# Block-sparse attention and a gated MLP on one core: another mask setup, and transposes, values and evictions of the first batch in other places

## The chip, the core and the metric

The kernel runs on one core of a Trainium2 chip. Its engines work side by side, each through its own instructions in order: TensorE (PE in the profile; its weight loads are PEld), VectorE (DVE), ScalarE (ACT), GpSimd (POOL) and SyncE (SP), whose queue issues most of the DMAs. An instruction that needs another engine's result waits on a semaphore, and all that is queued behind it on its engine waits too. The metric is the device time of one execution in microseconds (us), less being better.

## The reference

Attention over 4 batches of 8 heads, 768 positions, head size 64, with a mask of 24 x 24 blocks of 32 positions (the neighbours, the first and last rows and columns of blocks, and three sampled blocks in each row), and then a gated MLP with a product over the positions:

```python
scores = scale * np.matmul(q, k.transpose(0, 1, 3, 2))
scores = np.where(mask, scores, -1000000000.0)
...
x = softmax(scores) @ v            # heads side by side: batch, 768, 512
h = np.maximum(x @ w_in, 0.0)
u, v = h[..., :512], h[..., 512:]
v_n = (v - mean(v)) / np.sqrt(var(v) + 1e-06)
v_s = np.einsum('ts,bsd->btd', w_spatial, v_n) + b_spatial
return (u * v_s) @ w_out
```

## The kernel before

**The mask inside the product.** The tile `kq` holds, for each of 8 heads, keys and queries transposed: partitions 0 to 63 are the head's 64 numbers, partitions 64 to 87 (`MR`) are 24 rows of mask. In the key columns (`K_`) these rows are a one-hot of the key's block; in the query columns they hold 0 or -300 for each block. One product over 88 partitions so gives scores with the mask added. The query's mask rows are `bm` (24 x 24, written by DVE at L203) times the one-hot of the keys: `mask_rows` (L266) makes such a product of 256 columns, "a third", into PSUM, and copies it to head 0. `rows` (L233) copies mask rows from head 0 to other heads, on ACT, POOL or DVE.

**The front.** ACT and SP issue the first loads. PE runs 26 products on a tile of zeros (`filler`, L174), so that it is busy while the first keys come. DVE builds one-hot (L195, into head 0) and `bm`. ACT casts the first keys and copies the one-hot to heads 1 and 2. PE transposes the first keys of head 0 (`head`, L272), DVE copies them to `kq` (`split0`, L278), and the first queries of head 0 follow in the same way into `psq`. After that come the three mask products, m0, m1 and m2; m0 and m1 have as their moving operand whole columns of `kq`, so they wait for the keys' copies; m2 takes the 24 mask rows alone. ACT copies m0 and m1 out, DVE m2. 5, 2 and 1 fillers stand between (`FILL2`), and 5 more in slot 2 (`FILL3`).

**The stream.** `ORDER` (L302) is the order in which POOL casts the rest of batch 0: `k`, `q`, `v` and a number name the keys, queries or values of a pair of heads; a, b, c are the first third, the last two thirds or the last third of the queries; `r` stands for a copy of mask rows; w00 to w13 are pieces of w_in. SP issues the loads in the same order, four ahead. v3 stands behind q0c and q3b.

**The slots.** Batch 0 runs in 36 slots (`S0`). Slot 3u+e makes a piece of the scores of unit u: four products (L397) and one exponential on ACT (L402). Two PSUM tiles take turns for the scores. Units 0 and 1 are heads 0 and 1, units 2 to 4 the first query third of pairs 1 to 3, units 5 to 7 the second, units 8 to 11 the third. The product with the values (L443, eight matmuls for each slot) comes later: unit 2 in slots 10 to 12, unit 3 in 12 to 14, unit 4 in 15 to 17, unit 5 in 18 to 20. Its result stands in one of two PSUM tiles (tag `av`). DVE normalizes it (L425, L426), PE transposes it back into the same tile (`xtr_third`), and DVE copies it to `xt` (L208). Only then is the tile free, so the value product of unit 4 waits for the copy to `xt` of unit 2, and that of unit 5 for unit 3's.

Within a slot the order is scores, then what `pre` holds, value products, what `when` put there, MLP steps (`run_queue`), and what `late` holds. `tr_first(p)` transposes a pair's keys and its first query third (8 on PE, two copies of 1024 columns on DVE); `tr_rest(p)` does the other two thirds (4 on PE, two copies of 512 columns). They stand in slots 4, 6, 10 and in slots 8, 11, 15 for pairs 1, 2, 3. A copy of mask rows on DVE (heads 4 to 7, second and third query third) is in slot 14. From slot 36 on the other batches go through full heads (L410, L414, L461), with the MLP of the batch before in between (L547). The last product of a batch's MLP is copied out of PSUM by `o_product` (L640), ACT and DVE by turns, six copies in a batch.

Of the kernel before, what the change touches and what calls it, by code (L numbers as in the profile page):

```python
# [10 lines left out]
FP32 = mybir.dt.float32  # L11
# [3 lines left out]
ALU = mybir.AluOpType  # L15
# [11 lines left out]
def kernel(  # L27
# [16 lines left out]
    nc = tc.nc  # L44

    B, H, S, D = q.shape
    BLK = 32
    NB = S // BLK
    NR = sampled_blocks.shape[1]
    NCH = S // 128  # L50
# [10 lines left out]
    KR = D + NB  # L61
    NT = 3
    TC = NCH // NT
    TW = TC * 128
    S0 = NT * NG * 3
    FILL, FILL2, FILL3 = 26, (5, 2, 1), 5
    U_DVE = (0, 1, 2, 3, 4, 5)

    const = ctx.enter_context(tc.tile_pool(name="const", bufs=1))
# [1 line left out]
    psum = ctx.enter_context(tc.tile_pool(name="psum", bufs=1, space=bass.MemoryType.PSUM))  # L71
# [10 lines left out]
    kq = const.tile([KR, H, 2 * S], BF16, name="kq")  # L82
    NVV = 6
    vv = [const.tile([128, 2, NCH, VA], BF16, name=f"vv{s}") for s in range(NVV)]
    MR = slice(D, KR)
    K_, Q_ = slice(0, S), slice(S, 2 * S)

    def qcols(t0, n=1):
        return slice(S + t0 * TW, S + (t0 + n) * TW)
# [9 lines left out]
    H0, H1, BOTH = slice(0, 1), slice(1, 2), slice(0, 2)  # L99
# [16 lines left out]
    def cast(p, nm, eng, hs=BOTH, cs=ALLC):  # L116
        if nm == "v":
            dst = vv[p % NVV][:, hs, cs, 0:D]
        else:
            if p not in nat:  # L120
                nat[p] = work.tile([128, 2 * NCH, 2, D], BF16, tag="nat", bufs=4, name="nat")
            c0 = 0 if nm == "k" else NCH
            dst = nat[p][:, c0 + cs.start:c0 + cs.stop].rearrange("p c h d -> p h c d")[:, hs]
        src = st[nm, p].rearrange("p h (c d) -> p h c d", d=D)[:, hs, cs]
        if p == 0 and nm != "v":
            dst = nat0_view()[:, hs, (c0 + cs.start) * D:(c0 + cs.stop) * D]
            if cs is not C45:
                dst = dst[:, 0].rearrange("p (i t d) -> p t i d", t=2, d=D)
                src = src[:, 0].rearrange("p (t i) d -> p t i d", t=2)
            else:  # L130
                dst = dst.rearrange("p h (c d) -> p h c d", d=D)
        if eng is nc.scalar:
            nc.scalar.activation(out=dst, in_=src, func=AF.Copy)
        else:
            eng.tensor_copy(out=dst, in_=src)  # L135
# [13 lines left out]
    hot = const.tile([KR, NCH, 128], BF16)  # L149
    lim = const.tile([KR, NCH, 128], BF16)  # L150
    allow = const.tile([KR, NB], FP32)
    bm = const.tile([KR, 128], BF16)
# [15 lines left out]
    for s in range(NVV):  # L168
        nc.gpsimd.memset(vv[s][:, :, :, D:VA], 1.0)
    nc.gpsimd.memset(mhalf, -0.5)  # L170

    wps = psum.tile([128, 512], FP32, tag="av", bufs=2)

    def filler(n, to):  # L174
        for _ in range(n):
            nc.tensor.matmul(out=to[:, 0:128], lhsT=warm, rhs=warm, start=True, stop=True)
# [3 lines left out]
    def ts(out, in0, s1, o0, s2=None, o1=None):  # L180
        kw = {} if o1 is None else {"op1": o1}
        nc.vector.tensor_scalar(out=out, in0=in0, scalar1=s1, scalar2=s2, op0=o0, **kw)  # L182

    def tt_op(out, in0, in1, op):
        nc.vector.tensor_tensor(out=out, in0=in0, in1=in1, op=op)
# [6 lines left out]
    nc.vector.memset(band[MR, 0:1], 1.0)  # L192
    nc.vector.memset(band[MR, NB - 1:NB], 1.0)
    ts(lim[MR], hot[MR], 1.0 - BLK, ALU.max, BLK - 1.0, ALU.min)
    tt_op(kq[MR, 0, K_].rearrange("b (c p) -> b c p", c=NCH), hot[MR], lim[MR], ALU.is_equal)  # L195


    tt_op(eq[MR, 0:NR], col[MR],
# [6 lines left out]
    PL, DV = nc.gpsimd, nc.vector  # L205
# [4 lines left out]
    def act_copy(o, i):  # L210
        nc.scalar.activation(out=o, in_=i, func=AF.Copy)  # L211
# [11 lines left out]
    def w_in_cast(u, g, eng):  # L223
        eng.tensor_copy(out=w_in_t[:, g, 0 if u else DH:DH if u else DFF], in_=wst.pop((u, g)))
# [8 lines left out]
    def rows(hs, cs, eng=nc.vector):  # L233
        src = kq[MR, 0:1, cs].to_broadcast([NB, hs.stop - hs.start, cs.stop - cs.start])
        if eng is nc.scalar:
            nc.scalar.activation(out=kq[MR, hs, cs], in_=src, func=AF.Copy)
        else:
            eng.tensor_copy(out=kq[MR, hs, cs], in_=src)  # L238

    cast(0, "k", nc.scalar, H0, C03)  # L240
    rows(H1, K_, nc.scalar)
    rows(slice(2, 3), slice(0, 512), nc.scalar)
    cast(0, "q", PL, H0, C03)
    cast(0, "k", PL, H0, C45)
    cast(0, "k", PL, H1)
# [5 lines left out]
    def moe_tag():  # L251
        moe_tags.rotate(1)
        if moe_tags[0] in held:
            moe_tags.rotate(1)
        return moe_tags[0]

    def bank(nm="ps", tag=None):
        return psum.tile([128, 1024], BF16, tag=tag or moe_tag(), bufs=2 if tag else 1, name=nm)
# [4 lines left out]
    def pair_of(src, c):  # L263
        return src[:, c].rearrange("p h d -> p (h d)")

    def mask_rows(ps, t0, n, copy, rs=slice(0, KR)):  # L266
        nc.tensor.matmul(out=ps[:, 0:n * TW], lhsT=bm[rs],
                         rhs=kq[rs, 0, t0 * TW:(t0 + n) * TW], start=True, stop=True)
        return lambda: copy(kq[MR, 0, qcols(t0, n)], ps[0:NB, 0:n * TW])


    def head(ps, h, c0, n, at=0):  # L272
        for i in range(0, n, 2):
            nc.tensor.transpose(out=ps[:, at + i * 64:at + (i + 2) * 64],
                                in_=nat0_view()[:, h, (c0 + i) * D:(c0 + i + 2) * D],
                                identity=ident)

    def split0(ps, h, c0, n, t, copy=dve_copy):  # L278
        w = n * 64
        copy(kq[0:D, h, c0 * 128 + t * w:c0 * 128 + (t + 1) * w], ps[t * D:(t + 1) * D, 0:w])  # L280
# [4 lines left out]
    split0(ps0, 0, *K4, 0)  # L285
    split0(ps0, 0, *K4, 1)
    filler(FILL2[0], wps)
    psq = bank("psq", "av")
    head(psq, 0, *Q4)
    split0(psq, 0, *Q4, 0)  # L290
    filler(FILL2[1], wps)
    mask_rows(psum.tile([128, 1024], FP32, tag="sc", bufs=2, name="mq"), 0, 1, act_copy)()
    m1 = mask_rows(psum.tile([128, 512], FP32, tag=moe_tag(), bufs=1, name="mq"), 1, 1, act_copy)
    m2 = mask_rows(psum.tile([128, 1024], FP32, tag="sc", bufs=2, name="mq"), 2, 1, dve_copy, MR)
    filler(FILL2[2], wps)
    split0(psq, 0, *Q4, 1)
    m1()
    m2()
    rows(H1, qcols(0, NT), PL)
    rows(slice(2, 3), slice(512, S), PL)  # L300

    ORDER = ("q1a k1 v0 k2 q2a q1b v1 k3 q2b q3a v2 r q0c q3b v3 w00 w01 w02 w03 w10 w12 w11 w13").split()  # L302
    PIECE = {"k": ALLC, "v": ALLC, "a": C01, "b": C25, "c": C45, "q": ALLC}

    def stream(x, f, w):
        if x[0] == "w":
            w(int(x[1]), int(x[2]))
        elif x[0] != "r":
            f(int(x[1]), x[0], PIECE[x[2:] or x[0]])

    def ahead(x):
        stream(x, lambda p, nm, cs: load(p, nm, cs=cs), w_in_load)

    AHEAD = 4
    for x in ORDER[:AHEAD]:
        ahead(x)
    for i, x in enumerate(ORDER):
        stream(x, lambda p, nm, cs: cast(p, nm, PL, cs=cs), lambda u, g: w_in_cast(u, g, PL))
        if x == "r":
            rows(slice(2, 4), qcols(1, 2), PL)  # L320
        for y in ORDER[i + AHEAD:i + AHEAD + 1]:
            ahead(y)
    nc.sync.dma_start(out=b_col, in_=moe_b_spatial.rearrange("(p c) -> p c", c=NCH))
# [233 lines left out]
    class Moe:  # L557
# [82 lines left out]
        def o_product(self, tcc, n):  # L640
            steps = []
            osb = {}
            parts = 2 if self.last and n == NCH - 1 else 1
            w = DM // parts
            for i in range(parts):
                cs = slice(i * w, (i + 1) * w)

                def done(ps, i=i, cs=cs):
                    if i == 0:
                        osb["t"] = work.tile([128, DM], FP32, tag="osb", bufs=6, name="osb")  # L650
                    on_act = (n + i) % 2 == 0
                    (act_copy if on_act else dve_copy)(osb["t"][:, cs], ps)
                    (nc.scalar if i else nc.sync).dma_start(
                        out=out[self.b].rearrange("(p c) d -> c p d", c=NCH)[tcc][:, cs],
                        in_=osb["t"][:, cs])
                steps += product(NDH, lambda d: self.gt[:, tcc, d, :],
                                 lambda d, cs=cs: w_out_t[:, d, cs], self.last, done, w)
            return steps
# [40 lines left out]
    def when(slot, *fns):  # L699
        at.setdefault(slot, []).extend(fns)  # L700

    def c(f, *a, **kw):
        return lambda: f(*a, **kw)
# [8 lines left out]
        when(sl, c(tr_first, p))  # L712
    for sl, h0, h1, cs in ROWS:
        when(sl, c(rows, slice(h0, h1), cs))
    for p, sl in ((1, 8), (2, 11), (3, 15), (0, 18)):
        when(sl, c(tr_rest, p, 2 if p == 0 else 1))
    for u, slot in enumerate((13, 14, 15, 19, 22, 25, 28, 30, 34, 37, 40), 1):
        (pre if u == 2 else late).setdefault(slot, []).append(c(xtr_third, u))
# [146 lines left out]
```

## Time and profile before

| | us |
|---|---|
| three runs | 212.53, 212.55, 213.78 |
| median | 212.55 |
| the profiled execution | 213.05 |
| its span in the profile | 211.2 |

The span goes from the first to the last instruction that the profiler saw, and 1.85 us of the profiled execution lie around it. Times below are counted from the span's start. A row of the timeline gives start, length, engine, line, operation, what is written from what, and the number of instructions merged into it; in brackets stands the idle time of the engine ahead of it and what ended that. PE's lengths contain the way of the data through the array, so successive rows of PE overlap; the distance between starts is what one takes of the engine.

### The profile page before, as it was taken

How to read it: one execution, taken by the hardware profiler on the slowest of the kernel's cores; microseconds unless marked ns; L12 is line 12 of the kernel's file. 1: busy time of each engine (PE TensorE's matmuls, PEld its weight loads, DVE VectorE, ACT ScalarE, POOL GpSimd, SP SyncE). 2: the span in 40 equal slices, each digit the busy share in tenths (PEclk: the TensorE clock that was granted, in tenths of full speed). 3: DMA queues.
4: the chain of work that ended last, by engine and by line, in shares of the span. 5: the costliest groups of instructions: out<-in, count | busy, mean ns of one | idle time of the engine just before them, and what ended most of it. 6: DMA issues, size and time to landing. Idle time of an engine off the chain costs nothing.

```text
span 211.2 us, 5346 instructions
## 1 busy us (share of the span) xinstructions
PE 204.7 (97%) x2144; PEld 130.2 (62%) x2144; DVE 129.8 (61%) x289; ACT 169.5 (80%) x224; POOL 83.7 (40%) x182
## 2 busy tenths in 40 slices
PE   8899999999999999999999999999999999999992
PEld 7687878756666666665665666666665566544441
DVE  7699785999663543384975464284984443476551
ACT  5898999999999999978998888979889786275021
POOL 6786949965957825006159042006220000012000
PEclk9999999999999999999999999999999999999999
DMA  5999699999999989999955599489401225510285
GB/s 156 292 359 369 208 298 249 252 297 334 263 352 236 275 166 280 284 229 355 197 201 112 114 220 208 154 192 253 87 3 37 50 53 132 194 62 0 50 174 202
DMA packets 64685, 41.97 MB, mean 199 GB/s; under 512 B 45716, under 2 KB 59412, under 8 KB 64660
## 3 DMA queue, kind: packets, MB, share of 16 engines
q1 hardware_dynamic: 64228, 41.24, 76.1%
q10 hardware_dynamic: 432, 0.39, 0.6%
q8 instruction: 16, 0.26, 0.5%
q14 instruction: 9, 0.07, 0.1%
HBM read 24.38 MB, written 6.29 MB: 145 GB/s over the span
## 4 chain that ended last, share of the span: by engine, by line
PE 86%; DMA 8%; POOL 2%; SPq 1%; ACT 1%; issue 0%; ACTq 0%; POOLq 0%
PE ps_moe L547 33%; PE ps L410 22%; PE ps_av L461 13%; DMA st_v<-in_v_dram 7%; PE ps_t L547 7%; PE ps L397 4%; PE ps_sc L547 3%; PE ps_av L443 3%; SPq L107 1%; DMA out_dram<-osb 1%; POOL vv L135 1%; ACT osb L211 1%; POOL kq L238 0%; PE ps_av L261 0%; POOL nat L135 0%; PE ps L261 0%
## 5 line engine op out<-in xcount | busy, mean ns | idle before, releaser
L414 ACT ACTIVATE a_all<-ps 128x768 bf16<-128x768 f32 x144 | 113.7, 812 | 15.2 <-PE ps L410 7.1
L410 PE MATMUL ps<-kq 88*128 88x384 bf16 x288 | 70.5, 326 | 0.1
L461 PEld LDWEIGHTS <-a_all 128*128 128x128 bf16 x864 | 46.4, 97 | 20.0
L461 PE MATMUL ps_av<-vv,a_all 128*128 128x65 bf16 x864 | 51.2, 194 | 0.0
L410 PEld LDWEIGHTS <-kq 88*128 88x128 bf16 x288 | 28.0, 98 | 30.4 <-issue 0.5
L547 PE MATMUL ps_moe<-w_in_t,xt 128*128 128x512 bf16 x144 | 43.9, 378 | 0.0
L402 ACT ACTIVATE a_all<-ps 128x1024 bf16<-128x1024 f32 x36 | 34.5, 1027 | 1.8 <-PE ps L397 1.6
L135 POOL CAST nat<-st_k 128x256 bf16<-128x256 f32 (+3 forms) x37 | 15.9, 460 | 43.2 <-DMA st_k<-in_k_dram 30.9
L547 PE MATMUL ps_moe<-vn,w_spt 128*128 128x512 bf16 x108 | 32.7, 378 | 0.0
L615 DVE SCALAR_TENSOR_TENSOR un<-ps_moe,b_col,un 128x512 bf16<-128x512 f32 x18 | 13.5, 748 | 16.6 <-PE ps_moe L547 16.4
L397 PE MATMUL ps<-kq 88*128 88x256 bf16 (+1 forms) x140 | 21.6, 276 | 1.2 <-ACT a_all L402 0.6
L425 DVE RECIPROCAL rc<-ps_av 128x6 f32<-128x6 f32 (+1 forms) x36 | 6.6, 185 | 24.5 <-PE ps_av L461 22.9
L547 PE MATMUL ps_moe<-w_out_t,gt 128*128 128x512 bf16 x72 | 21.5, 378 | 0.0
L584 POOL TENSOR_SCALAR std<-mv 128x3 f32<-128x3 f32 (+1 forms) x9 | 2.1, 238 | 48.2 <-DVE mv L581 35.3
L135 POOL CAST nat<-st_q 128x256 bf16<-128x256 f32 (+2 forms) x41 | 19.1, 495 | 2.7 <-DMA st_q<-in_q_dram 2.4
L135 POOL CAST vv<-st_v 128x256 bf16<-128x256 f32 (+1 forms) x36 | 17.4, 514 | 5.8 <-DMA st_v<-in_v_dram 3.5
L547 PEld LDWEIGHTS <-xt 128*128 128x128 bf16 x192 | 15.2, 97 | 7.0 <-DVE xt L208 0.2
L426 DVE TENSOR_TENSOR xn<-ps_av,rc 128x384 bf16<-128x384 f32 (+1 forms) x36 | 18.5, 513 | 1.2
L580 DVE BATCH_NORM_STATS2 stats<-vn 128x6 f32<-128x512 bf16 x24 | 16.5, 689 | 1.5 <-ACT vn L575 0.9
L182 DVE TENSOR_SCALAR vn<-ps_moe 128x512 bf16<-128x512 f32 x18 | 12.3, 684 | 6.0 <-PE ps_moe L547 6.0
L397 PEld LDWEIGHTS <-kq 88*128 88x128 bf16 x140 | 12.6, 97 | 4.8 <-DVE kq L208 1.1
L443 PE MATMUL ps_av<-vv,a_all 128*128 128x65 bf16 x288 | 14.8, 194 | 0.2 <-POOL vv L135 0.2
(84 smaller groups left out, 210.6 us busy)
## 6 DMA issues: line engine op xcount, KB each, us to landing
st_v<-in_v_dram SPq DMA_DIRECT2D x16, 384.0 KB, 6.5
out_dram<-osb SPq DMA_DIRECT2D x23, 256.0 KB, 2.6
st_k<-in_k_dram SPq DMA_DIRECT2D x15, 384.0 KB, 3.9
st_q<-in_q_dram SPq DMA_DIRECT2D x12, 384.0 KB, 4.7
ws_f<-in_moe_w_spatial_dram SPq DMA_DIRECT2D x6, 384.0 KB, 5.5
w_f<-in_moe_w_in_dram SPq DMA_DIRECT2D x8, 256.0 KB, 7.2
w_f<-in_moe_w_out_dram SPq DMA_DIRECT2D x4, 256.0 KB, 4.7
st_q<-in_q_dram SPq DMA_DIRECT2D x3, 256.0 KB, 7.1
```

The source lines that it names most:

```text
L135: eng.tensor_copy(out=dst, in_=src)
L182: nc.vector.tensor_scalar(out=out, in0=in0, scalar1=s1, scalar2=s2, op0=o0, **kw)
L397: nc.tensor.matmul(out=ps[:, at:at + n * TW], lhsT=kq[:, h, ci * 128:(ci + 1) * 128], rhs=kq[:, h, qcols(t0, n)], start=True, stop=True)
L402: nc.scalar.activation(out=out, in_=ps, func=AF.Exp, scale=0.125)
L410: nc.tensor.matmul(out=ps[:, hf * 512:hf * 512 + HALF], lhsT=kq[:, j % H, ci * 128:(ci + 1) * 128], rhs=kq[:, j % H, S + hf * HALF:S + (hf ...
L414: nc.scalar.activation(out=a_ref["h", j][:, ci, :].rearrange("p (b c) -> p b c", b=2), in_=ps.rearrange("p (b c) -> p b c", b=2)[:, :, 0:H ...
L426: nc.vector.tensor_tensor(out=out, in0=ps[:, :, 0:D], in1=rc[:, 0:n].to_broadcast([128, n, D]), op=ALU.mult)
L443: nc.tensor.matmul(out=av_ref[u][:, to, :], lhsT=a_ref[u][:, at:at + 128], rhs=vv[pp % NVV][:, h, ci, :], start=(ci == 0), stop=(ci == NCH ...
L461: nc.tensor.matmul(out=av_ref[j][:, qc, :], lhsT=a_ref["h", j][:, ci, qc * 128:(qc + 1) * 128], rhs=vv[p % NVV][:, h, ci, :], start=(ci == ...
L547: nc.tensor.matmul(out=ref["ps"][:, 0:w], lhsT=lhs(i), rhs=rhs(i), start=(i == 0), stop=(i == n - 1))
L580: nc.vector.bn_stats(out=stats, in_=self.vn[:, tcc, :])
L615: nc.vector.scalar_tensor_tensor(out=self.un[:, tcc, :], in0=ps, scalar=b_col[:, tcc:tcc + 1], in1=self.un[:, tcc, :], op0=ALU.add, op1=AL ...
```

## The change

- **Mask.** DVE writes the one-hot into head 1 instead of head 0. POOL zeroes the first 256 key columns of head 1, partitions 0 to 63, so that m0 can be made from head 1 without any keys. m0 now stands behind two fillers, ahead of the queries' transposes. ACT copies the one-hot from head 1 to head 0 before that, and to head 2 after m0's eviction. m1 follows the queries and is made from head 0 as before, evicted by ACT at once. m2 moves to slot 3, on all 88 partitions, evicted by DVE there.
- **Mask rows.** The copies of the last third to heads 1, 2 and 3 come out of the early copies on POOL (768 to 512 columns for head 1, 2 x 512 to 2 x 256 for `r`) and become one copy of 3 x 256 in slot 16, behind the casts of w_in in POOL's order.
- **Fillers.** 2, 2, 2 instead of 5, 2, 1, and 3 instead of 5 in slot 2.
- **Order.** v3 moves ahead of q3b and q0c, in POOL's casts and in SP's loads; q3b now comes ahead of q0c.
- **Transposes.** `tr_rest(1)` moves from slot 8 to 11, `tr_rest(2)` from 11 to 13.
- **Evictions.** `o_product` gives all six copies of batch 0 to DVE (three of them were ACT's).

```diff
-    FILL, FILL2, FILL3 = 26, (5, 2, 1), 5
+    FILL, FILL2, FILL3 = 26, (2, 2, 2), 3
...
+    nc.gpsimd.memset(kq[0:D, 1, 0:TW], 0.0)
...
-    tt_op(kq[MR, 0, K_].rearrange("b (c p) -> b c p", c=NCH), hot[MR], lim[MR], ALU.is_equal)
+    tt_op(kq[MR, 1, K_].rearrange("b (c p) -> b c p", c=NCH), hot[MR], lim[MR], ALU.is_equal)
...
-    rows(H1, K_, nc.scalar)
-    rows(slice(2, 3), slice(0, 512), nc.scalar)
+    act_copy(kq[MR, 0, K_], kq[MR, 1, K_])
...
-    def mask_rows(ps, t0, n, copy, rs=slice(0, KR)):
-        nc.tensor.matmul(out=ps[:, 0:n * TW], lhsT=bm[rs],
-                         rhs=kq[rs, 0, t0 * TW:(t0 + n) * TW], start=True, stop=True)
-        return lambda: copy(kq[MR, 0, qcols(t0, n)], ps[0:NB, 0:n * TW])
+    def mask_rows(ps, t, copy, h=0):
+        nc.tensor.matmul(out=ps[:, 0:TW], lhsT=bm, rhs=kq[:, h, t * TW:(t + 1) * TW],
+                         start=True, stop=True)
+        copy(kq[MR, 0, qcols(t)], ps[0:NB, 0:TW])
...
     filler(FILL2[0], wps)
+    mask_rows(psum.tile([128, 1024], FP32, tag="sc", bufs=2, name="mq"), 0, act_copy, 1)
+    rows(slice(2, 3), slice(0, 512), nc.scalar)
+    filler(FILL2[1], wps)
     psq = bank("psq", "av")
     head(psq, 0, *Q4)
     split0(psq, 0, *Q4, 0)
-    filler(FILL2[1], wps)
-    mask_rows(psum.tile([128, 1024], FP32, tag="sc", bufs=2, name="mq"), 0, 1, act_copy)()
-    m1 = mask_rows(psum.tile([128, 512], FP32, tag=moe_tag(), bufs=1, name="mq"), 1, 1, act_copy)
-    m2 = mask_rows(psum.tile([128, 1024], FP32, tag="sc", bufs=2, name="mq"), 2, 1, dve_copy, MR)
     filler(FILL2[2], wps)
+    mask_rows(psum.tile([128, 512], FP32, tag=moe_tag(), bufs=1, name="mq"), 1, act_copy)
     split0(psq, 0, *Q4, 1)
-    m1()
-    m2()
-    rows(H1, qcols(0, NT), PL)
+    rows(H1, qcols(0, 2), PL)
     rows(slice(2, 3), slice(512, S), PL)
-    ORDER = ("q1a k1 v0 k2 q2a q1b v1 k3 q2b q3a v2 r q0c q3b v3 w00 w01 w02 w03 w10 w12 w11 w13").split()
+    ORDER = ("q1a k1 v0 k2 q2a q1b v1 k3 q2b q3a v2 r v3 q3b q0c w00 w01 w02 w03 w10 w12 w11 w13").split()
...
-            rows(slice(2, 4), qcols(1, 2), PL)
+            rows(slice(2, 4), qcols(1), PL)
...
-                    on_act = (n + i) % 2 == 0
+                    on_act = self.b > 0 and (n + i) % 2 == 0
...
-    for p, sl in ((1, 8), (2, 11), (3, 15), (0, 18)):
+    when(3, lambda: mask_rows(psum.tile([128, 512], FP32, tag=moe_tag(), bufs=1, name="mq"), 2, dve_copy))
+    when(16, lambda: rows(slice(1, 4), qcols(2), PL))
+    for p, sl in ((1, 11), (2, 13), (3, 15), (0, 18)):
```

## The prediction

> **What bounds the kernel now.** I read the page first: busy shares, then the chain of work that ended last.
>
> ```profile
> span 211.2 us, 5346 instructions
> PE 204.7 (97%) x2144; PEld 130.2 (62%) x2144; DVE 129.8 (61%) x289; ACT 169.5 (80%) x224; POOL 83.7 (40%) x182
> PE 86%; DMA 8%; POOL 2%; SPq 1%; ACT 1%; issue 0%; ACTq 0%; POOLq 0%
> ```
>
> PE is the bound, and the chain runs on it for 86% of the span. All of the DMA's share but a little lies in one place, which the chain in order of time shows (start, length, what):
>
> ```profile
> 9.29 8.17 DMA st_v<-in_v_dram
> 17.46 0.05 issue
> 17.52 0.83 POOL vv L135
> 18.41 1.04 POOL kq L238
> ...
> 20.46 0.78 POOL vv L135
> 21.29 0.41 PE ps_av L443 x8
> ```
>
> The values v2 land at 17.46, POOL casts them by 18.35, and v3's cast, behind other work on POOL, lets PE go on at 21.29. From there PE never rests for long. So a cut before 17.5 is worth only what is left of it once v2 and what follows it have been waited for. I therefore went through the timelines of PE, DVE and POOL from the front to slot 18, and then to the one later place that the diff touches.
>
> **The front.** PE, ACT, DVE, POOL by the timeline:
>
> ```profile
> 0.97 2.95 PE L176 MATMUL wps<-warm 128*128 128x128 bf16 x26 [0.97 <-DVE tiny L155]
> 3.72 0.42 PE L274 MATMUL ps<-ident,nat 128*128 128x128 bf16 x2
> 4.89 0.42 PE L267 MATMUL mq<-kq,bm 88*128 88x256 bf16 x1
> 5.86 0.68 PE L397 MATMUL ps<-kq 88*128 88x256 bf16 x4
> ...
> 3.45 1.36 ACT L236 ACTIVATE kq<-kq 24x768 bf16<-24x768 bf16 x2
> 5.35 0.64 ACT L211 ACTIVATE kq<-mq 24x256 bf16<-24x256 f32 x2 [0.54 <-PE mq L267]
> 6.57 11.35 ACT L402 ACTIVATE a_all<-ps 128x1024 bf16<-128x1024 f32 x12 [0.58 <-PE ps L397]
> ...
> 3.74 0.29 DVE L182 TENSOR_SCALAR bm<-allow 24x24 bf16<-24x24 f32 x1
> 4.92 0.61 DVE L208 COPY kq<-psq 64x256 bf16<-64x256 bf16 x2
> 10.56 1.41 DVE L208 COPY kq<-ps 64x1024 bf16<-64x1024 bf16 x2 [0.94 <-PE ps L261]
> ...
> 3.61 0.40 POOL L135 CAST nat<-st_q 128x256 bf16<-128x256 f32 x1 [0.43 <-DMA st_q<-in_q_dram]
> ```
>
> A filler takes (3.72 - 0.97)/26 = 0.106, a product of 256 columns twice that, 0.21. The keys' two transposes end their turn at 3.93, two fillers at 4.14; `bm` is there at 4.03, so m0 runs 4.14 to 4.56 (0.42 to its result; before it started at 4.89). ACT's 1.36 covers 768 and 512 columns, about 0.8 and 0.55; it now does the 768 first, is free at 4.25, copies m0 out in 0.32 by 4.9, does the 512 by 5.5 and m1 by 5.8. PE: two fillers to 4.57, the queries' transposes to 4.78 with their result near 5.0, two fillers, m1 to 5.2. DVE copies the first query columns 5.0 to 5.35, and the first scores start at 5.4, against 5.86. Still at 0.21 for 256 columns they give the first exponential near 6.2, against 6.57: **0.35 us earlier**.
>
> The rest of the front costs nothing. POOL's memset of 64 x 256 has no row of its own; between nothing and the 0.43 that POOL idles before 3.61 it is hidden, and even 0.4 more would end the query cast at 4.4, ahead of the 4.57 at which its transposes stand. m2 in slot 3 adds 0.11 of PE, where ACT sets the pace, and one copy of 0.4 on DVE, which idles 0.94 before 10.56. Slot 2's two fillers less were not waited for by anything.
>
> **Slots 4 to 12: the lead grows, then goes.** ACT runs twelve exponentials without a gap from 6.57, so all of this moves with the 0.35 until data stop it:
>
> ```profile
> 14.59 1.28 POOL L135 CAST nat<-st_q 128x512 bf16<-128x512 f32 x2
> ...
> 17.07 2.29 DVE L208 COPY kq<-ps 64x1024 bf16<-64x1024 bf16 x4
> ...
> 17.80 0.61 PE L397 MATMUL ps<-kq 88*128 88x256 bf16 x4 [0.46 <-DVE kq L208]
> 18.25 0.68 PE L443 MATMUL ps_av<-vv,a_all 128*128 128x65 bf16 x16
> 18.76 0.60 PE L397 MATMUL ps<-kq 88*128 88x256 bf16 x4
> 19.20 0.42 PE L443 MATMUL ps_av<-vv,a_all 128*128 128x65 bf16 x8
> 19.45 0.39 PE L261 MATMUL ps<-ident,xn 128*128 128x128 bf16 x4
> ```
>
> Slot 12's scores at 17.80 wait for `tr_first(3)` on DVE, which starts at 17.07 because `tr_rest(1)` stood ahead of it. With that moved to slot 11, `tr_first(3)` is bound by its query cast, which ends at 14.59 + 1.28 = 15.87: two transposes later DVE starts near 16.2, head 6 is there at 16.9, and the scores start at 17.0, **0.8 us earlier**. `tr_first(3)` and then `tr_rest(1)` end at 17.6 and 18.5.
>
> But of slot 12's sixteen value products the second eight are unit 3's and need v2. They ran at 18.25 + 0.25 = 18.50, 0.15 behind the cast's end of 18.35. Now PE comes there at 17.7 and waits until 18.40. Of the 0.8, **0.1 is left**.
>
> **Slots 13 to 18: DVE gives it back.** From 18.40: unit 3's eight 0.25, scores 0.44 (18.76 to 19.20), eight more 0.25, and now `tr_rest(2)`, four transposes at 0.22 (19.45 to 19.68), starting at 19.35, result near 19.75. DVE by its timeline:
>
> ```profile
> 19.94 0.42 DVE L208 COPY xt<-ps 128x512 bf16<-128x512 bf16 x1
> 20.43 0.29 DVE L208 COPY xt<-ps_av 128x256 bf16<-128x256 bf16 x1
> 20.68 0.18 DVE L425 RECIPROCAL rc<-ps_av 128x4 f32<-128x4 f32 x1
> ...
> 21.36 0.98 DVE L238 COPY kq<-kq 24x2048 bf16<-24x2048 bf16 x1
> 22.36 0.85 DVE L208 COPY kq<-ps 64x512 bf16<-64x512 bf16 x2
> 23.25 0.29 DVE L208 COPY xt<-ps_av 128x256 bf16<-128x256 bf16 x1
> ...
> 21.29 0.41 PE L443 MATMUL ps_av<-vv,a_all 128*128 128x65 bf16 x8 [0.17 <-POOL vv L135]
> ...
> 24.13 0.42 PE L443 MATMUL ps_av<-vv,a_all 128*128 128x65 bf16 x8
> ```
>
> Before, `tr_rest(2)` was copied by 17.07 + 2.29 = 19.36, ahead of unit 2's normalization. Now that comes first (DVE is through with it by 19.2, as `tr_rest(1)` ended at 18.5) and DVE then idles until 19.8. After it: `tr_rest(2)` 0.85, `xt` of unit 1 0.42, `xt` of unit 2 0.29, with 0.03 between: 21.4, where before it was 20.72. Unit 4's value products need that PSUM tile, so they start at 21.45; v3 is no longer what they wait for (its cast follows half as large a mask copy; even in its old place it ended at 21.24). Against 21.29: **+0.16**. DVE goes on with unit 3's normalization 0.65, the mask copy 0.98, `tr_rest(3)` 0.85, `xt` of unit 3 0.29, and gaps: 24.25, so unit 5's value products start at 24.3 against 24.13; PE's own 2.84 from 21.45 says 24.29. Two counts agree, and +0.16 goes on into PE's stream, which has no gap to swallow it.
>
> POOL's new copy of 3 x 256 is about 0.8 by 1.04 for its 2 x 512; it stands behind the last w_in cast, where POOL has idled waiting for the next keys, and its reader is slot 24. Nothing.
>
> **Batch 0's evictions.** ACT, DVE, PE in slots near 80:
>
> ```profile
> 78.27 0.59 ACT L211 ACTIVATE osb<-ps_moe 128x512 f32<-128x512 f32 x1
> ...
> 78.40 1.13 DVE L208 COPY kq<-tt 64x1536 bf16<-64x1536 bf16 x2
> 80.55 0.69 DVE L208 COPY osb<-ps_moe 128x512 f32<-128x512 f32 x1 [1.02 <-PE ps_moe L547]
> ...
> 79.19 0.38 PE L547 MATMUL ps_moe<-w_out_t,gt 128*128 128x512 bf16 x1
> 79.61 0.48 PE L410 MATMUL ps<-kq 88*128 88x384 bf16 x2
> ```
>
> A 512-column product takes PE 0.215 (twice the 0.11 of a warm 256), so the scores at 79.61 came 0.21 late: ACT had put 0.59 of eviction ahead of an exponential. On DVE the eviction costs 0.69, fits with the 1.13 before 80.55 (1.02 of idle), and the tile is free before its next product. The other two evictions delayed nothing on PE. **-0.21**. SP's output DMAs wait for DVE in place of ACT; they were issued later than either ended.
>
> **Sum.** +0.16 - 0.21 = -0.05: the profiled execution's 213.05 becomes 213.0. It lies 0.5 above the median of 212.55; on that scale the forecast is 212.5.
>
> **Rivals.**
> *A, v2 lands early (faster).* Its 8.17 from issue to landing may hold a delay that comes and goes from run to run. If it landed 1 us earlier, unit 3's products start by 17.7, DVE is then bound by its own queue (`tr_rest(2)` right behind the normalization, 19.2), `xt` of unit 2 ends at 20.75, and unit 4 starts at 20.8: -0.5, with the eviction -0.7, 211.85. Against it: no transfer ahead of v2 changes, and SP issues v2 on the landing of v0. Chance 0.25, with lesser gains in it.
> *B, DVE's backlog (slower).* If `tr_first(3)` starts on DVE no earlier than the 17.07 of before (late casts, or `rows` and normalizations ahead of it), `tr_rest(1)` ends at 19.35, unit 2's normalization 20.0, and everything down to unit 4 comes at 21.7: +0.4, in all +0.2, 212.75. The point that decides is a start at 16.85; each 0.1 later adds 0.1, and at 17.7 it is 213.4. For it: three DVE copies now meet in slots 10 to 13. Chance 0.22.
> *C, PE stays at half speed longer (slower).* The page's granted clock does not show it, but the rows do: a 128-column product takes 0.106 in the fillers and 0.055 in the four transposes at 19.45. If the four fillers that are gone kept PE slow for another 3 us, PE's work there doubles, at worst +3 in its turn, less the 0.8 of lead and the waits for ACT: +1, 213.3. Against it: PE's queue stays full to 5.2 and stalls only 0.2. [...] Chance 0.06.
> *D, the eviction's gain does not come*, since the scores at 79.61 wait for something else as late: +0.2, 212.7. Chance within the forecast's.
>
> **Chances and range.** The forecast with D has 0.47, from 212.2 to 212.9: my starts are good to some 0.15 each. Over 1% is 2.1 us, about what a measurement of this kernel tells from no change. All of PE's visible waits between 5.86 and 21.29 and at 79.61 do not add up to that, so faster by it has 0.06, for a mechanism that I do not see. Slower by it needs C at its worst or a new wait in the gapless stretch: 0.13. The range takes in A's 211.85 and B's 213.4 and some of the spread of the runs before (212.53 to 213.78): 211.4 to 213.9.
>
> **What would show it.** First scores near 5.4 and first exponential near 6.2; slot 12's scores near 17.0, unit 3's value products near 18.4 on POOL's cast; DVE idle before `tr_rest(2)`, unit 4's products at 21.45 released by DVE, not POOL; no gap at 79.6; from 25 on all of PE's rows shifted by one amount. I am wrong if v2 lands elsewhere than 17.46, if unit 4 is released by POOL, or if PE shows new gaps after 25.

## The result, and the profile after

| | before | after |
|---|---|---|
| median of 22 runs each, us | 212.84 | 212.00 |
| lowest to highest, us | 212.03 to 213.82 | 211.43 to 214.36 |
| time of the profiled execution, us | 213.05 | 211.45 |
| its span, us | 211.2 | 209.4 |

The ratio of after to before is 0.9965, with a 95% interval of 0.9949 to 0.998: 0.35% less, or 0.74 us of 212.84 (0.43 to 1.09). The two profiled executions differ by more, 1.8 us of span, so part of what the two profiles show is chance. The page of after:

```profile
span 209.4 us, 5342 instructions
...
PE 203.5 (97%) x2140; PEld 129.3 (62%) x2140; DVE 131.5 (63%) x292; ACT 168.7 (81%) x221; POOL 85.0 (41%) x184
...
PE 90%; ACT 5%; DMA 2%; DVE 1%; issue 0%; ACTq 0%; POOL 0%
```

PE is still the bound. In the chain of waits DMA has gone from 8% to 2%, and POOL from 2% to nothing. The chain in order of time says where (start, length, what):

```profile
1.15 2.79 DMA st_q<-in_q_dram
...
5.76 8.50 ACT a_all L400 x9
...
18.19 0.42 DVE xn L424
18.61 0.32 DVE kq L209
18.95 0.43 DVE kq L209
19.41 0.63 DVE xt L209 x2
20.09 0.43 PE ps_av L441 x8
```

The 8.17 us of v2's load and the two value casts are not in it any more. ACT's exponentials set the pace up to 14.26, PE's own stream from there to 18, and then DVE leads to unit 4's value products: normalization, `tr_rest(2)` (two copies to `kq`), two copies to `xt`. The timeline of POOL, DVE and PE there:

```profile
15.36 0.83 POOL L135 CAST vv<-st_v 128x768 bf16<-128x768 f32 x1 [0.17 <-DMA st_v<-in_v_dram]
...
15.64 2.29 DVE L209 COPY kq<-ps 64x1024 bf16<-64x1024 bf16 x4
18.53 0.85 DVE L209 COPY kq<-ps 64x512 bf16<-64x512 bf16 x2
19.41 0.42 DVE L209 COPY xt<-ps 128x512 bf16<-128x512 bf16 x1
19.75 0.28 DVE L209 COPY xt<-ps_av 128x256 bf16<-128x256 bf16 x1
...
16.38 0.61 PE L395 MATMUL ps<-kq 88*128 88x256 bf16 x4
20.09 0.43 PE L441 MATMUL ps_av<-vv,a_all 128*128 128x65 bf16 x8 [0.20 <-DVE xt L209]
```

v2's cast starts at 15.36, where it started at 17.52 in the profile before. Slot 12's scores (16.38) wait for nothing, where before they waited 0.46 for DVE. Unit 4's products wait 0.20 for DVE's copy of unit 2 to `xt`, as the prediction had it, and not for POOL.

The evictions of batch 0, in the timeline of ACT, DVE and PE:

```profile
76.40 3.18 ACT L412 ACTIVATE a_all<-ps 128x768 bf16<-128x768 f32 x4 [0.20 <-PE ps_av L459]
...
77.24 0.68 DVE L209 COPY osb<-ps_moe 128x512 f32<-128x512 f32 x1
77.83 1.43 DVE L209 COPY kq<-tt 64x1536 bf16<-64x1536 bf16 x2
...
78.02 0.38 PE L545 MATMUL ps_moe<-w_out_t,gt 128*128 128x512 bf16 x1
78.24 0.49 PE L408 MATMUL ps<-kq 88*128 88x384 bf16 x2
```

ACT runs four exponentials in a row, the copy to `osb` is on DVE, and PE goes from the MLP product to the next scores in 0.22, where before it took 0.42 (79.19 to 79.61).

The end holds the part that the prediction did not have. The last output DMA, from the timeline of before, then of after, and after's row of the DMA issues (its last column: us from issue to landing):

```profile
207.65 0.35 ACTq L653 DMA_DIRECT2D out_dram<-osb  x1
```

```profile
206.28 0.35 ACTq L651 DMA_DIRECT2D out_dram<-osb  x1
```

```profile
out_dram<-osb ACTq DMA_DIRECT2D x1, 128.0 KB, 2.1
```

The transfer takes 2.1 in both. From the issue to the end of the span it is 211.2 - 207.65 = 3.55 before and 209.4 - 206.28 = 3.12 after. The landings, which the trace has to the hundredth, give 1.41 from the last landing to the end before, and 0.99 after: 0.42 us less, in a stretch where no engine computes.

So the two spans differ by 1.12 at slot 18's scores (23.70 and 22.58), 0.25 on PE from there to its last instruction (206.87 and 205.50), and 0.43 behind that. Slot 18's scores in the timeline of PE, before, then after:

```profile
23.70 0.60 PE L397 MATMUL ps<-kq 88*128 88x256 bf16 x4
```

```profile
22.58 0.60 PE L395 MATMUL ps<-kq 88*128 88x256 bf16 x4
```

The experiments ask which of these three belong to the change.

### The profile page after: what moved, and what is told of

Same layout as the page of the kernel before. It is cut to its first block, busy times and chain, and to the rows that moved or that the text cites. A ratio compares the mean times of both kernels' runs of the same rounds, so it can differ in the third digit from the quotient of the medians.

```text
span 209.4 us, 5342 instructions
## 1 busy us (share of the span) xinstructions
PE 203.5 (97%) x2140; PEld 129.3 (62%) x2140; DVE 131.5 (63%) x292; ACT 168.7 (81%) x221; POOL 85.0 (41%) x184
## 4 chain that ended last, share of the span: by engine, by line
PE 90%; ACT 5%; DMA 2%; DVE 1%; issue 0%; ACTq 0%; POOL 0%
PE ps_moe L545 33%; PE ps L408 22%; PE ps_av L459 13%; PE ps_t L545 7%; PE ps L395 5%; ACT a_all L400 4%; PE ps_av L441 4%; PE ps_sc L545 3%; DMA st_q<-in_q_dram 1%; DMA out_dram<-osb 1%; PE ps L261 1%; PE ps_av L261 1%; DVE kq L209 0%; ACT osb L212 0%; DVE xt L209 0%
## 5 line engine op out<-in xcount | busy, mean ns | idle before, releaser
L459 PE MATMUL ps_av<-vv,a_all 128*128 128x65 bf16 x864 | 51.2, 194 | 0.0
L135 POOL CAST nat<-st_k 128x256 bf16<-128x256 f32 (+3 forms) x37 | 16.6, 481 | 43.4 <-DMA st_k<-in_k_dram 30.6
L135 POOL CAST vv<-st_v 128x256 bf16<-128x256 f32 (+1 forms) x36 | 18.1, 534 | 3.8 <-DMA st_v<-in_v_dram 3.8
L135 POOL CAST nat<-st_q 128x256 bf16<-128x256 f32 (+2 forms) x41 | 18.1, 472 | 0.9 <-DMA st_q<-in_q_dram 0.6
L209 DVE COPY kq<-tt 64x1536 bf16<-64x1536 bf16 x24 | 14.9, 619 | 0.3
```

The source lines that it names most:

```text
L209: nc.vector.tensor_copy(out=o, in_=i)
L459: nc.tensor.matmul(out=av_ref[j][:, qc, :], lhsT=a_ref["h", j][:, ci, qc * 128:(qc + 1) * 128], rhs=vv[p % NVV][:, h, ci, :], start=(ci == ...
```

## The experiments

Each kernel ran 11 or 12 times beside 34 or 35 runs of the kernel before on the same chip; ratios are to that.

### The kernel before, once more

No edit. Its purpose was the scatter of the front.

> The kernel before, unchanged, to see how much its front differs from one profile to the next. If the time at which PE reaches full speed and the landing of v2 are properties of the program, PE is slow until 5.8 us again and v2 lands near 17.5 (within 0.2), with unit 3's value products at 18.5 and unit 5's at 24.1. If they are a matter of chance, as the profile of after (full speed by 3.7, v2 at 15.3) lets suspect, one of them differs here by 0.5 us or more and the span with it. Ratio to itself: 1.000 within 0.002.

Ratio 0.9994 (0.9976 to 1.0013). Its profile is another one in the front, by the timeline of POOL, then of PE:

```profile
16.00 0.83 POOL L135 CAST vv<-st_v 128x768 bf16<-128x768 f32 x1 [0.17 <-DMA st_v<-in_v_dram]
...
5.49 0.60 PE L397 MATMUL ps<-kq 88*128 88x256 bf16 x4
20.36 0.42 PE L443 MATMUL ps_av<-vv,a_all 128*128 128x65 bf16 x8
```

v2's cast starts 1.5 earlier than in the first profile of the same kernel, the first scores 0.37 earlier, and unit 4's products, 0.93 earlier, wait for nobody. In all the profiles but that first one v2's cast starts between 15.25 and 16.62. From issue to landing v2's load took 6.05 to 6.75 in those thirteen, and 8.17 in the first. **The 17.46 on which the prediction built was that one execution's.**

### The mask setup alone

Before with the new mask setup, the copies of mask rows and the fillers; the order of the casts, the transposes and the evictions stay as they were.

```diff
+    mask_rows(psum.tile([128, 1024], FP32, tag="sc", bufs=2, name="mq"), 0, act_copy, 1)
...
+    when(3, lambda: mask_rows(psum.tile([128, 512], FP32, tag=moe_tag(), bufs=1, name="mq"), 2, dve_copy))
+    when(16, lambda: rows(slice(1, 4), qcols(2), PL))
```

> The kernel before with the new mask setup, mask rows and fillers alone (old stream order, old transposes, old evictions). Theory 1 (the prediction's: v2's landing takes the lead away): first exponential 0.35 us earlier than in before, slot 12 still bound by tr_first(3) behind tr_rest(1) on DVE, unit 4's products within 0.1 of before, time ratio 0.999 to 1.001. Theory 2 (the lead goes through ACT's row of exponentials and v2 is not the bound in most runs): unit 5's products earlier by the whole lead of the first exponential, ratio 0.997 to 0.9985.

Ratio 0.9994 (0.9973 to 1.0014), median 212.89. The timeline of PE and ACT:

```profile
3.72 0.42 PE L274 MATMUL ps<-ident,nat 128*128 128x128 bf16 x2
4.15 0.42 PE L267 MATMUL mq<-kq,bm 88*128 88x256 bf16 x1
5.37 0.82 PE L395 MATMUL ps<-kq 88*128 88x256 bf16 x4
6.03 0.22 PE L274 MATMUL ps<-ident,nat 128*128 128x128 bf16 x1
...
6.22 3.77 ACT L400 ACTIVATE a_all<-ps 128x1024 bf16<-128x1024 f32 x4 [0.40 <-PE ps L395]
```

PE runs slow until 5.8 here (the fillers ahead of 3.72 are 0.106 apart), as in the first profile of before. m0 at 4.15, the first scores at 5.37 and the first exponential at 6.22 are the prediction's 4.14, 5.4 and 6.2. The gain of 0.35 at the first exponential is there; in the time it is not seen. Slot 12 still waits 0.47 for DVE, as the first theory said, but unit 4's products start at 20.61 and not within 0.1 of 21.29, since v2 does not hold them up here.

### The moved transposes alone

```diff
-    for p, sl in ((1, 8), (2, 11), (3, 15), (0, 18)):
+    for p, sl in ((1, 11), (2, 13), (3, 15), (0, 18)):
```

> The kernel before with the transposes of pairs 1 and 2 moved to slots 11 and 13 alone. Theory 1: slot 12's scores come up to 0.8 us earlier, v2 takes most of that, DVE's copies for unit 4 come 0.2 later than before: ratio 1.000 to 1.002. Theory 2: slot 12 no longer stalls and 0.3 to 0.5 us stay in the stream: ratio 0.998 to 0.999.

Ratio 1.0006 (0.9983 to 1.0029), median 212.96. The timeline of DVE, then PE:

```profile
19.47 0.85 DVE L208 COPY kq<-ps 64x512 bf16<-64x512 bf16 x2
20.69 0.28 DVE L208 COPY xt<-ps_av 128x256 bf16<-128x256 bf16 x1
...
21.03 0.43 PE L443 MATMUL ps_av<-vv,a_all 128*128 128x65 bf16 x8 [0.19 <-DVE xt L208]
```

The wait for DVE at unit 4 comes with the move of `tr_rest(2)` and needs nothing else of the change.

### The evictions alone

```diff
-                    on_act = (n + i) % 2 == 0
+                    on_act = self.b > 0 and (n + i) % 2 == 0
```

> The kernel before with batch 0's six output copies on DVE alone. Both theories: the scores near 79.6 no longer stall by 0.21 us, nothing else moves; ratio 0.999 (0.998 to 1.000). If the stall only changes its place, the ratio is 1.000 and a gap of 0.2 shows elsewhere between 78 and 90 us.

Ratio 0.9967 (0.9945 to 0.9989), median 212.14: **this one line gives what the whole change gives** (0.9965), as near as the runs can tell. Its timeline of PE near 78, and its end:

```profile
78.27 0.38 PE L547 MATMUL ps_moe<-w_out_t,gt 128*128 128x512 bf16 x1
78.48 0.49 PE L410 MATMUL ps<-kq 88*128 88x384 bf16 x2
```

```profile
core 0 of [0], span 209.6 us
...
206.52 0.35 ACTq L653 DMA_DIRECT2D out_dram<-osb  x1
```

From the product to the scores it is 0.21, from issue to end 3.1, both as in after. So it has both the 0.2 on PE and the 0.4 at the end.

### After with the old evictions

```diff
-                    on_act = self.b > 0 and (n + i) % 2 == 0
+                    on_act = (n + i) % 2 == 0
```

> The changed kernel with the evictions of batch 0 as before (ACT and DVE by turns): mask setup, order and transposes alone. If the whole gain is the evictions' (0.26 us on PE near 80 and 0.43 us behind the last output's landing), this is as fast as before: ratio 0.999 to 1.001, and its end (last landing to the end of the span) is 1.4 us as before and not 1.0. If mask setup and moves carry the gain, the ratio is 0.997 to 0.998.

Ratio 0.9986 (0.9963 to 1.0009), median 212.64. PE's timeline has the gap again:

```profile
78.56 0.38 PE L545 MATMUL ps_moe<-w_out_t,gt 128*128 128x512 bf16 x1
78.99 0.49 PE L408 MATMUL ps<-kq 88*128 88x384 bf16 x2
```

0.43 from the product to the scores. From the last landing to the end it is 1.41 again. What the rest of the change is worth is not told from nothing: 0.30 us less than before, between 0.79 less and 0.19 more.

### One more DMA on SP

Why would the end depend on the evictions? SP's program has 211 instructions before and 210 after: with the output DMAs waiting for DVE in place of ACT it has one instruction less that waits for a semaphore (71 after, 72 before). This kernel is after with one small load added to SP, late in the kernel, into a tile that nobody reads.

```diff
+    extra0 = const.tile([KR, 2 * NR], I32)
...
+    when(150, lambda: nc.sync.dma_start(out=extra0[MR], in_=_listify(sampled_blocks).bitcast(I32)))
```

> The changed kernel with one more small load (24 x 6 numbers, read by nobody) in SP's queue at slot 150, far from any bound: SP's program is one instruction longer, as long as before's (211 against 210). Theory S: at the end a pause of 0.36 us sits at a fixed place of SP's program and the eviction change moved it behind a step where it is hidden; then the end is 1.4 us again and the time is 0.4 us over after's (ratio to before 0.998 to 0.999). Rival: the shorter end comes with the evictions or the output DMAs themselves; then the end stays at 1.0 and the ratio at 0.9965.

Ratio 0.9982 (0.9964 to 0.9999), median 212.43. Its timeline at the end:

```profile
core 0 of [0], span 211.2 us
...
207.71 0.35 ACTq L652 DMA_DIRECT2D out_dram<-osb  x1
```

3.5 from issue to end, and 1.50 from the last landing to the end. The load itself is issued at 147.69, some 60 us ahead of that. With 211 instructions on SP the lost 0.4 to 0.5 is back in the profile, though the evictions are on DVE. The time alone would not show it: the interval holds after's 0.9965.

### Fewer instructions on SP, before and after

If the length of SP's program sets the end, two instructions less should move it too. SP's own last output DMA, the last but one of all, goes to ACT's queue; the same edit in before and in after:

```diff
-                    (nc.scalar if i else nc.sync).dma_start(
+                    (nc.scalar if i or (self.last and n == 3) else nc.sync).dma_start(
```

> The kernel before with one output DMA of the last batch (the fourth tile) issued by ACT, which is idle there, in place of SP: SP's program is shorter by one or two instructions (211 before), nothing else changes. Theory S (a pause of 0.36 us at a fixed place of SP's program): it leaves the place between SP's last two drains, and the span from the last DMA's issue to its end, 3.2 us in before, falls by up to 0.43 if the pause then stands where POOL's steps hide it; ratio 0.998. Rival (the short end belongs to the evictions): 3.2 us stay, ratio 1.000.

> The changed kernel with the same output DMA on ACT: SP's program one or two instructions under 210. If the pause moves on behind the end altogether, the end falls below after's 2.76 us from the last issue and the ratio to before is 0.995; if it comes to stand in front of a later step that the end waits for, the end is 2.8 to 3.1; if program length is not the cause, 2.76.

Before with it: ratio 1.0005 (0.9984 to 1.0025). After with it: 0.9961 (0.9939 to 0.9983). The expectations count from the end of the last issue, 0.35 or so behind its start: 3.2 in before and 2.76 in after. By that measure before with fewer keeps its 3.2, and its ratio is 1.000, as the rival had it; after with fewer has 3.0. But the stretch contains the landing, and here that comes later: SP's last output is now issued 0.03 behind ACT's last, and lands last, 2.36 after its issue. Before, ACT's landed last, 2.13 after its issue. Behind the landing before with fewer is shorter, 1.25 in place of 1.41. All the profiles together, from the landing of the last output to the end of the span:

| instructions on SP | kernels | us from last landing to end | SP's 208th instruction |
|---|---|---|---|
| 211 | before (two profiles), mask setup alone, transposes alone, after with the old evictions | 1.41 to 1.43 | the drain ahead of the first common step |
| 211 | after with one more DMA | 1.50 | the same |
| 210 | after (two profiles), evictions alone, three more kernels with the new evictions | 0.99 to 1.00 | the wait for the first common step |
| 209 | before with fewer | 1.25 | the drain ahead of the second common step |
| 208 | after with fewer | 1.02 | the wait for the second common step, the last of all |

Eleven profiles with 210 or 211 split without an exception (twelve with the added DMA), and the added DMA sets the evictions apart from the count. It is no steady price by the instruction, since 209 lies between.

What the length decides can be read from the trace, which holds SP's waits too, though the views leave them out. After the waits for the last landings SP executes two drains (DRAIN in the trace). Then come two common steps of SP, ACT, DVE and POOL: for each, the others execute a drain that raises a semaphore POOL waits for, and then wait for a semaphore that POOL raises. Somewhere in this SP pauses. Counted from its first instruction, the 208th starts 0.35 to 0.39 behind the end of the 207th in all 14 profiles, **at the same place of the program, whatever its length**. What differs is which instruction stands there:

- With 211 it is the second drain (the two drains start at 210.01 and 210.37 before), so POOL and with it the others wait for it.
- With 210 it is the wait behind that drain (the drains start at 208.62 and 208.67 after, the wait at 209.06). The other engines got POOL's answer by 208.84 and went on meanwhile, so the pause costs little: 0.99 is no more than the 1.02 with 208.
- With 209 it is the drain ahead of the second step, and a part of the pause shows.
- With 208 it is the last wait, which is 0.39 behind its predecessor in any case, as it is with 211: a pause there would be hidden, and isn't told from that wait.

The 1.50 of the added DMA has 0.06 more between landing and first drain, and 0.03 more in the pause. What SP does in the pause stays open. A packet of 8 KB, of the kind that the trace calls instruction, starts 0.6 to 0.9 us behind the 208th instruction in every profile, and none lies in the pause; whether the two have to do with each other was not tried.

### The transposes of pairs 2 and 3 later

Two ways to keep DVE free for unit 2's copy to `xt`. First after with `tr_rest(2)` in slot 14:

```diff
-    for p, sl in ((1, 11), (2, 13), (3, 15), (0, 18)):
+    for p, sl in ((1, 11), (2, 14), (3, 15), (0, 18)):
```

> The changed kernel with tr_rest(2) in slot 14 instead of 13, so that its two copies (0.85 us) stand behind the copy to xt of unit 2 on DVE. If DVE's queue is what takes the lead of slot 12 away again (unit 4's products released by DVE in after and moves_alone), unit 4 is no longer released by DVE and comes 0.3 to 0.45 us earlier after slot 13 than in after; ratio 0.9945 to 0.996. Rival: another wait takes its place (the values, or unit 5's tile in slot 18), and the ratio stays at 0.9965.

Ratio 0.9974 (0.996 to 0.9989), median 212.24. The timeline of PE, then of DVE:

```profile
20.97 0.42 PE L441 MATMUL ps_av<-vv,a_all 128*128 128x65 bf16 x8
23.14 0.38 PE L545 MATMUL ps_moe<-w_in_t,xt 128*128 128x512 bf16 x1 [0.72 <-DVE kq L209]
...
21.18 0.95 DVE L239 COPY kq<-kq 24x2048 bf16<-24x2048 bf16 x1
22.14 1.74 DVE L209 COPY kq<-ps 64x512 bf16<-64x512 bf16 x4
```

Unit 4 waits for nothing now. But `tr_rest(2)` falls behind the mask copy (0.95) on DVE, its PSUM tile is held until then, and the first MLP product waits 0.72. A wait was removed and a longer one took its place.

With `tr_rest(3)` in slot 16 as well:

```diff
+    for p, sl in ((1, 11), (2, 14), (3, 16), (0, 18)):
```

> As later_pair2, and tr_rest(3) in slot 16 instead of 15, behind the copy to xt of unit 3: unit 5's tile is free 0.85 us earlier on DVE. If unit 5's products were the next to wait for DVE, this gains over later_pair2 by 0.1 to 0.4 us; if they were not, the two are equal within 0.1.

Ratio 0.9974 (0.9952 to 0.9995), median 212.41; the first MLP product waits 0.60 here. The two are equal as far as the runs tell, and neither beats after.

### After once more, and after with the old transposes

The first without an edit, the second:

```diff
-    for p, sl in ((1, 11), (2, 13), (3, 15), (0, 18)):
+    for p, sl in ((1, 8), (2, 11), (3, 15), (0, 18)):
```

> The changed kernel, unchanged, for a second profile of its front. Unit 4's products are released by DVE again, the end is 1.0 us from the last landing. The first exponential lies between 5.7 (PE at full speed by 4) and 6.3 (full speed near 6). Ratio 0.9965, 0.995 to 0.998 as before.

> The changed kernel with the transposes of pairs 1 and 2 back in slots 8 and 11; mask setup, order and evictions new. If the moves take away slot 12's stall and give the same back at unit 4 (from first exponential to unit 4's products 14.3 us in after and moves_alone, 14.2 to 14.5 in the kernels with the old places), this is as fast as after: ratio 0.996 to 0.997, with unit 4 not released by DVE and slot 12 released by DVE. If the moves are worth anything in the stream, it is 0.3 us slower than after (0.998).

After: 0.9939 (0.9916 to 0.9963), median 211.89; unit 4's products wait for DVE again, the first exponential starts at 6.01, and the end is 0.99 behind the last landing. With the old transposes: 0.9955 (0.9926 to 0.9985), median 211.98. The kernel before ran 0.4 slower beside these (213.18) than beside the others (212.79 to 212.84); after's own median is 0.1 from its first. The moves make no difference that can be told. The timeline of PE with the old transposes has slot 12's wait again, and none at unit 4:

```profile
17.57 0.61 PE L395 MATMUL ps<-kq 88*128 88x256 bf16 x4 [0.18 <-DVE kq L209]
...
20.71 0.42 PE L441 MATMUL ps_av<-vv,a_all 128*128 128x65 bf16 x8
```

From the first exponential to unit 4's products it is 14.32 to 15.07 in the six profiles with the moves as in the change, and 14.23 to 14.98 in the six without them. That way contains the scatter of the front. From slot 11's scores, behind the scatter, to slot 18's it is 7.13 or 7.14 in five of the six with the moves (7.41 in the sixth), and 6.75 to 6.83 in four of those without; in the other two of these (7.12 and 7.45), slot 12 waited nearly 0.5 for DVE. So the moves cost PE 0.3 to 0.4 there, except where that long wait is taken away.

## Why the prediction was right, and where it was wrong

**The time.** Forecast 212.5, or 0.05 less than before; measured 212.0 and 0.74 less (0.43 to 1.09). Inside the range and within 1%, but the sum was not right: it lacked the larger of the two terms that the runs show. The range, 211.4 to 213.9, is wide enough to hold no change at all, so that it holds the result says little. The direction, down, came from the one term that was right.

**Right: the evictions, -0.21.** From slot 18's scores to PE's last instruction it is 183.13 to 183.17 in five of the six profiles with the old evictions (183.39 in before's second), and 182.92 to 182.94 in all eight with the new. Rival D, that this gain does not come, is out.

**Wrong: "SP's output DMAs wait for DVE in place of ACT; they were issued later than either ended."** The step weighed when the DMAs start and counted nothing. But the waits are instructions of SP's program, and one less of them shifts what falls on the pause behind the 207th: the kernel ended 0.42 earlier behind its last landing. The profile's rows showed no work at the end, so no term stood for it: -0.21 - 0.42 = -0.63, which the evictions alone bear out (0.33% of 212.79 is 0.70, between 0.23 and 1.17). That the new length was a good one is luck: with 209 the stretch was 1.25.

**Wrong: v2 lands at 17.46, so of slot 12's lead 0.1 is left.** The prediction called itself wrong if v2 landed elsewhere, and in after it landed at 15.30. No other profile shows it as late as 17.46. In the thirteen others nothing on PE waits for v2, and the chain of before, with its 8.17 for v2's load, was that of an unlucky execution. Rival A had named the delay as one that comes and goes, and A's picture came: `tr_rest(2)` right behind the normalization, unit 4 released by DVE. But before has the early v2 as well, and then also goes faster, so A's 0.5 is no gain of the change: in the second profile of each, slot 18's scores stand at 22.77 before and 22.82 after, so the 1.12 between the first two profiles is no sign of the change. That the median came within 0.2 of A's 211.85 is not for A's reason.

**Right: DVE gives the lead back.** Unit 4's products wait 0.19 or 0.20 for the copy to `xt` in all six profiles with the moves as in the change. Slot 12's scores follow slot 11's by 0.94 or 0.95 in five of them (1.22 in the sixth) and by 1.18 to 1.55 without the moves: that is the lead, 0.23 to 0.61. From slot 13's scores to unit 4's products it is 2.74 to 2.75 with the moves and 2.18 to 2.20 in the five profiles without that v2 does not hold up: 0.55 is given back, nearly the most that the slot gains, and more than it gains in four of the six. About 0.2 of it is PE's own: `tr_rest(2)`'s transposes now stand there (18.04 to 18.26 in after). With them, but without the wait for DVE, it is 2.38 (`tr_rest(2)` in slot 14), so DVE's part is 0.36. The step, +0.16 at unit 4, had the direction right. Its size was counted from the late v2. From slot 11's scores to unit 4's products it is 4.64 or 4.65 in five of the six with the moves and 4.33 to 4.41 in four without: there the moves cost some 0.3. In the other two without (4.70 and 5.04) slot 12's long wait had come first. In the time it is not seen.

**Right as a row, not seen in the time: the front, -0.35.** Where PE was slow until 5.8, the rows came as worked out (6.22 against 6.57). Where PE was at full speed sooner, the old front was fast too (the first exponential at 5.97 in before with fewer SP instructions, PE at full speed from 4.14; the new one had 5.78 in after with the old evictions, from 3.93), and 0.2 of the lead was left. From the first exponential to slot 18's scores, the kernels with the old placement or the change's scatter from 16.6 to 17.6, so 0.35 at the start isn't found at slot 18. Whether a part of it reaches the end is open: the interval of the mask setup alone (0.57 less to 0.30 more) holds it, and holds zero as well.

**Rivals B and C.** `tr_first(3)` starts on DVE at 15.64 in after, far from B's 16.85, and from 15.89 to 16.82 in four of the other five profiles with the moves. In the fifth, after with one more DMA, it is 17.08, with no idle time on DVE ahead of it: B's picture, with unit 4's products at 21.51. C, fewer fillers that keep PE slow, did not show in the time, which fell. Its 3 us more of slow PE were the author's supposition, and no run shows them: PE's full speed begins from 3.72 to 6.73 us in nine profiles with the new fillers and from 4.14 to 5.78 in five with the old, too few to tell a later start from scatter. The new place of v3 was not tried alone; in no profile but the first of before did PE wait for v3's cast.

## What to carry to other kernels

Before a sum is built on a landing time in one profile, look whether a second profile of the same kernel has it: here the load that led the chain of waits was late in one profile of the fourteen taken. Copies that moved to another engine here changed the waits of the DMA queue that reads their result, and SP's program went from 211 to 210 instructions, so look at what the waits do to the length of SP's program as well as at when its transfers start, and compare the end of the kernel, behind the last landing, in the profiles before and after. And where a stall is taken away by moving work on an engine that runs in order, follow that engine's queue to its next reader: three placements of the same transposes gave waits in three places and no difference in time that could be told.

## What the runs showed of the hardware

- **The end of the program depends on SP's program length.** It is 1.41 us or 0.99 from the last landing to the end, by one instruction in 211; it was 1.50 with 211 by another way, 1.25 with 209 and 1.02 with 208. SP's 208th instruction starts 0.35 to 0.39 behind the end of its 207th in all 14 profiles, and the length decides who waits for it.
- **PE's full speed begins at a different time in each execution.** It was 5.78 and 4.52 in two profiles of before, 3.72 and 4.79 in two of after, 6.73 at the latest, seen by the distance of products, which falls from 0.106 to 0.055 for 128 columns. It lies 1.3 and 1.1 us apart in two executions of one kernel, and 3.0 over all 14. What sets it is not shown.
- **A load of the front can land late in one execution alone.** v2's load took 6.05 to 6.75 us from issue to landing in thirteen profiles and 8.17 in one; with the scatter of its issue, its cast starts between 15.25 and 17.52. In the late profile a 16 KB packet of the kind instruction took 1.17 us (14.42 to 15.59) while the load was under way. But such a packet is in every profile near that time, and with the transposes alone one of 1.20 (14.68 to 15.88) lay inside a load of 6.59. So the packet by itself doesn't make the load late; what did stays open.
